# The first 28 slices of a fused attention and gated feed-forward kernel in another hand-given order, with another ring of PSUM banks

## The chip, the cores and the metric

The kernel runs on one core of one Trainium2 chip, as one launch. The metric is the device time of the execution in microseconds (us); lower is better. The core has TensorE (PE, its weight loads shown as PEld), VectorE (DVE), ScalarE (ACT), GpSimd (POOL) and SyncE (SP). Each runs its own instructions in its own order, and they wait for each other by semaphores.

## The reference

```python
# x: [8, 8, 512, 64], state: [8, 8, 32, 64]
scores  = x @ state^T / 8;  a  = softmax(scores);   xread = a @ state     # per batch and head
scores2 = state @ x^T / 8;  a2 = softmax(scores2);  sread = a2 @ x
t = concat([xread, sread], axis=2)        # [8, 8, 544, 64], then heads side by side: [4352, 512]
out = (relu(t @ w_gate) * (t @ w_val)) @ w_out      # 512 -> 1536 -> 512
```

## The kernel before

Matmuls take bf16 and accumulate in the eight PSUM banks (numbers 0 to 7, one tile of 128x512 each). The rows of `xread` are never formed. For each batch the kernel computes U, the product of the state with `w_gate` and `w_val`, and multiplies it by the transposed attention weights (ANS).

The work is cut into **slices**: slice (b, jf) is batch b of 8 and block jf of 12 of the hidden width. A slice is four matmuls of 512 columns into two banks (`gv`, line 290: gate and value), a relu on ACT (line 314), and a multiply on DVE (line 318) that writes `h_sb`. The output projection of a batch is cut into 12 pieces of four matmuls (`out_mms`, line 327); three pieces make one output tile of 128 rows, which ACT copies out of its bank (`fin_x`, line 335) and SP writes to memory (line 339).

**Two ways to set the order.** From slice (2, 4) on, a loop writes the order: a slice, its relu and multiply, one output piece that lags by 18 slices, and then whatever `at` has put behind that slice. For batch 3 that is: the scores of its first heads behind slice (2, 4) and of the others behind (2, 5), U in two blocks behind (2, 7) and (2, 10). The first 28 slices, all that leads up to them and ten output pieces are one long string of words, `program` (line 409). Each word calls one step with its numbers, and each engine meets the instructions in the order of the words. The digits behind `@` are the PSUM banks that the step takes. Steps of the loop take banks from a ring of six (`bank`, line 81), output tiles from banks 6 and 7 in turn.

The words used below (b is a batch):

- `dx.b.part.parts`, `dw`, `ds`, `do`: loads of x, of columns of `w_gate` (dw.0) and `w_val` (dw.1), of the state and of `w_out`, all issued by POOL. The second half of batch 0 is loaded by POOL ahead of the list (line 387), its first half by SP and ACT.
- `xc`, `stc`: casts; `stT`, `sto`: transposed state and its eviction.
- `xT.b.lo.n`, `xo.b.lo.n.engine`: n transposes of blocks of x on PE, and their eviction.
- `sc.b.jp`, `ex`, `nr`, `nx`: scores of half the heads (line 170), exp on ACT (line 177), row sums and reciprocal on DVE (lines 183, 185), scaling on DVE (line 189).
- `aT.b.kc`, `ao`: the attention weights transposed on PE, and evicted to ANS (line 219).
- `c.b.lo.n`, `co.b.lo.n.kc.engine`: U for n columns (tile `upc`) and its evictions (line 285); `u`, `uo`: the same for 512 columns (tile `up`, line 275).
- `gv.b.jf`, `re`, `mu`: the three parts of a slice; `o.0.i`: output piece i of batch 0; `of.0.t`: `fin_x` of its tile t.
- `xd.b` and `ad.b`: the same transposes by DMA, issued by SP: x of batch b into `xT` (line 148), and the attention weights of batch b into ANS (line 197).
- `sr`, `sn`: the matmuls of `sread` (line 233) and their scaling; `xp.b`: POOL's copy of x of batch b into `xa` (line 225), which `sr` reads; `on`: the column of ones there.
- `spin.n.cols`: n matmuls of constants that nobody reads.

Behind the list, the loop's SP steps are transposes of the state (line 122) and of `sn` (line 246); POOL copies the former into `stT` (line 130) ahead of the load of batch 4.

Of the kernel before, what the change touches and what calls it, by code (L numbers as in the profile page):

```python
# [16 lines left out]
def kernel(  # L17
# [51 lines left out]
    stT = const.tile([128, 2, B, H, Ns], BF16, name="stT")  # L69
# [6 lines left out]
    xf, xb, xT, e_sn, a_sn, ANS, U, hsb, sr_sb = {}, {}, {}, {}, {}, {}, {}, {}, {}  # L76
    copy = {"act": nc.scalar.copy, "dve": nc.vector.tensor_copy, "pool": nc.gpsimd.tensor_copy}

    given, turn = [], {"r": 0, "o": 0}

    def bank(name, kind="r"):

        if given:
            n = given.pop(0)
        elif kind == "spare":
            n = 6 + turn["o"] % 2
        else:
            n = (4, 3, 2, 1, 0, 5)[turn["r"] % 6] if kind == "r" else 6 + turn["o"] % 2
            turn[kind] += 1
        return psum.tile([128, 512], FP32, name=name, tag=f"b{n}")  # L90

# [22 lines left out]
    def state_T(g):  # L114
        ps = held["st", g] = bank("stT_ps").bitcast(BF16)[:, 0:512]
        for i in range(4):
            nc.tensor.transpose(ps.rearrange("p (q i m) -> p q i m", i=4, m=8)[:, :, i],
                                st_b[:, g % 3, i].rearrange("p h d -> p (h d)"), id128)
# [31 lines left out]
    def x_T(b, lo, n):  # L150

        if b not in xT:
            xT_alloc(b)
        ps = held["xT", b, lo] = bank("xT_ps").bitcast(BF16)[:, 0:128 * n].rearrange("p (k t) -> p k t", t=128)
        for k in range(n):
            nc.tensor.transpose(ps[:, k], x_blocks(b)[:, lo + k], id128)  # L156
# [5 lines left out]
    def att_sc(b, jp):  # L162
        if b not in e_sn:
            e_sn[b] = att.tile([128, 2, NC, NJ * Ns], BF16, name="e_sn", tag="e_sn", bufs=4)
            a_sn[b] = att.tile([128, 2, NC, NJ * Ns], BF16, name="a_sn", tag="a_sn")
        t = held["sc", b, jp] = bank("sc_ps")
        ps = t.rearrange("p (r c j n) -> p r c j n", r=2, c=NC, j=2)
        for h in range(4 * jp, 4 * jp + 4):
            for k in range(2):
                nc.tensor.matmul(ps[:, h % 2, 2 * k:2 * k + 2, h // 2 % 2], xT[b][:, 2 * h + k], stT[:, :, b, h],  # L170
                                 start=True, stop=True)
# [235 lines left out]
             "c": c_unit, "co": c_out, "u": u_unit, "uo": u_out, "gv": gv, "re": relu, "mu": mult, "o": out_part,  # L407
             "of": fin_x, "xd": x_trans_dma, "ad": att_aT_dma, "xp": x_pad, "sr": sr_mm, "sn": sr_norm}
    program = """
    dx.1.0.2 dx.1.1.2 stc.0.1.dve stc.0.0.dve dw.0.0.128 dw.1.0.128 dw.0.128.128 dw.1.128.128 dw.0.256.256  # L410
    dw.1.256.256 dw.0.512.256 spin.8 stT.0@0 dw.1.512.256 dw.0.768.256 dw.1.768.256 dw.0.1024.256 dw.1.1024.256
    dw.0.1280.256 dw.1.1280.256 dx.2.0.1 ds do.0.6 xc.0.0.act spin.1.256 xT.0.0.4@1 xc.0.1.dve sto.0.0.act
    spin.1.128 xT.0.4.4@2 xo.0.0.4.dve sto.0.1.dve xo.0.4.4.act spin.1 sc.0.0@3 ex.0.0 nr.0.0 spin.1.256 spin.1.128
    xT.0.8.4@4 xT.0.12.4@5 xo.0.8.4.act xo.0.12.4.act spin.1 xT.1.0.8@6 sc.0.1@1 ex.0.1 xo.1.0.8.dve spin.1
    sc.1.0@0 xT.1.8.8@2 stc.1.1.pool stc.1.0.pool do.6.12 spin.1 c.0.0.128@34 nx.0.0 ex.1.0 nr.0.1 xo.1.8.8.act on
    stc.2.0.pool stc.3.1.pool co.0.0.128.0.act co.0.0.128.1.act spin.1 sc.1.1@5 nx.0.1 nr.1.0 aT.0.1@6 aT.0.0@1
    ex.1.1 c.1.128.128@02 ao.0.0.dve ao.0.1.act c.0.128.128@34 c.1.0.128@51 co.0.128.128.0.act gv.0.0@63
    co.1.128.128.1.act co.0.128.128.1.act re.0.0 co.1.128.128.0.act gv.0.1@72 nr.1.1 nx.1.0 co.1.0.128.1.act re.0.1
    nx.1.1 aT.1.0@4 aT.1.1@6 c.0.256.256@01 co.1.0.128.0.dve ao.1.0.dve c.1.256.256@57 co.0.256.256.0.act
    co.1.256.256.0.act co.1.256.256.1.act ao.1.1.dve co.0.256.256.1.dve gv.1.0@46 re.1.0 mu.0.0 mu.0.1 gv.0.2@01  # L420
    gv.1.2@53 mu.1.0 re.0.2 c.0.512.256@72 c.1.512.256@40 re.1.2 mu.1.2 co.0.512.256.1.dve mu.0.2 gv.1.3@65
    gv.1.1@32 co.1.512.256.1.act re.1.3 co.0.512.256.0.act re.1.1 co.1.512.256.0.dve gv.0.3@06 gv.1.5@17 mu.1.1
    mu.1.3 re.0.3 re.1.5 gv.1.4@34 mu.0.3 c.0.768.256@02 re.1.4 mu.1.5 c.0.1024.256@51 c.1.768.256@63
    co.0.768.256.0.act co.0.768.256.1.act mu.1.4 co.1.768.256.1.dve co.1.768.256.0.dve gv.0.4@74 gv.0.6@02 re.0.4
    co.0.1024.256.0.act re.0.6 gv.0.7@37 co.0.1024.256.1.dve mu.0.4 re.0.7 mu.0.6 gv.1.7@65 mu.0.7 re.1.7
    c.0.1280.256@10 c.1.1024.256@43 c.1.1280.256@26 mu.1.7 co.1.1280.256.1.act co.0.1280.256.0.act
    co.0.1280.256.1.dve co.1.1024.256.1.act co.1.1280.256.0.dve gv.0.9@75 co.1.1024.256.0.act gv.0.8@60 gv.0.5@12
    re.0.5 re.0.9 xT.2.0.8@3 re.0.8 mu.0.5 xT.2.8.8@4 xo.2.0.8.dve stT.1@1 sto.1.1.act xo.2.8.8.dve sto.1.0.act
    gv.0.11@72 re.0.11 mu.0.11 mu.0.8 gv.1.9@63 gv.1.11@41 re.1.9 mu.1.9 gv.0.10@76 gv.1.6@20 re.1.11 re.0.10
    sc.2.1@4 gv.1.10@73 re.1.10 ex.2.1 re.1.6 mu.0.10 mu.0.9 o.0.3@6 sc.2.0@5 o.0.4 ex.2.0 o.0.0@7 mu.1.10 mu.1.11  # L430
    u.2.1.1024@43 mu.1.6 nr.2.1 uo.2.1.1024.1.act u.2.1.0@21 u.2.1.512@50 uo.2.1.512.1.act uo.2.1.1024.0.act
    uo.2.1.512.0.act uo.2.1.0.0.act nx.2.1 uo.2.1.0.1.dve o.0.1 o.0.5 stc.2.1.pool dx.3.0.1 xp.1 xp.0 xd.3 sr.1@3
    stc.3.0.pool nr.2.0 sr.0@0 nx.2.0 sn.1 u.2.0.0@14 ad.2 of.0.1.act u.2.0.1024@52 u.2.0.512@63 o.0.2 of.0.0.act
    uo.2.0.0.0.act uo.2.0.512.1.act uo.2.0.512.0.dve o.0.6@6 o.0.7 o.0.9@7 o.0.8 of.0.2.act sn.0 gv.1.8@01
    uo.2.0.0.1.dve uo.2.0.1024.0.dve gv.2.0@45 re.2.0 re.1.8 mu.1.8 gv.2.2@36 xp.3 gv.2.3@40 re.2.2 re.2.3 xp.2
    gv.2.1@31 re.2.1 mu.2.1 mu.2.3 mu.2.0 uo.2.0.1024.1.act mu.2.2
    """
    for word in program.split():
        word, _, banks = word.partition("@")
# [107 lines left out]
```

## Time and profile before

| | |
|---|---|
| three runs | 220.83, 221.51, 221.74 us; median 221.51 |
| profiled execution | 221.39 us, of which the span of the profile is 219.6 us |
| granted TensorE clock, mean | 0.999 |
| PE, DVE, ACT, POOL busy in the span | 97%, 59%, 56%, 19% |
| share of the chain that ended last | PE 92%, DMA 3%, DVE 3% |
| of it, by line | out pieces L327 39%, slices L290 38% |

Times in the profile are microseconds from the start of the span. A PE row such as "x4" merges four matmuls; its length holds the drain of the last, so the time until the next row starts is what the group takes in PE's queue. Four matmuls of a slice or of an output piece take 0.86 us that way. In the chain, each piece is followed back to what released it, and "issue" is time in which an engine waited for nothing that the profile shows. A DMA has two lengths: that of the instruction on the engine that issues it, and the time until its data has landed.

### The profile page before, as it was taken

How to read it: one execution, taken by the hardware profiler on the slowest of the kernel's cores; microseconds unless marked ns; L12 is line 12 of the kernel's file. 1: busy time of each engine (PE TensorE's matmuls, PEld its weight loads, DVE VectorE, ACT ScalarE, POOL GpSimd, SP SyncE). 2: the span in 40 equal slices, each digit the busy share in tenths (PEclk: the TensorE clock that was granted, in tenths of full speed). 3: DMA queues.
4: the chain of work that ended last, by engine and by line, in shares of the span. 5: the costliest groups of instructions: out<-in, count | busy, mean ns of one | idle time of the engine just before them, and what ended most of it. 6: DMA issues, size and time to landing. Idle time of an engine off the chain costs nothing.

```text
span 219.6 us, 4861 instructions
## 1 busy us (share of the span) xinstructions
PE 214.0 (97%) x1957; PEld 105.5 (48%) x1957; DVE 129.4 (59%) x229; ACT 122.8 (56%) x235; POOL 41.7 (19%) x59
## 2 busy tenths in 40 slices
PE   8799999999999999999999999999999999999995
PEld 3454454454444444444444444444444445666544
DVE  5599978862987567665766487648675333222100
ACT  4699887746666565555566555746654544222222
POOL 7874059072143500040003000000000000000000
PEclk9999999999999999999999999999999999999999
DMA  7999999772949883655352105501411122222132
GB/s 164 166 194 198 196 235 174 115 195 81 134 90 145 161 140 96 143 98 102 86 133 79 51 19 142 119 16 48 102 49 54 48 48 49 51 49 74 70 95 99
DMA packets 42215, 23.65 MB, mean 108 GB/s; under 512 B 22640, under 2 KB 37872, under 8 KB 42192
## 3 DMA queue, kind: packets, MB, share of 16 engines
q0 software_dynamic: 16896, 9.05, 30.9%
q1 hardware_dynamic: 24400, 13.54, 23.5%
q10 hardware_dynamic: 896, 0.75, 1.3%
q8 instruction: 15, 0.25, 0.5%
q14 instruction: 8, 0.07, 0.1%
HBM read 18.35 MB, written 8.91 MB: 124 GB/s over the span
## 4 chain that ended last, share of the span: by engine, by line
PE 92%; DMA 3%; DVE 3%; issue 1%; POOL 0%; DVEq 0%; POOLq 0%
PE o_ps L327 39%; PE gv_ps L290 38%; PE gv_ps L307 5%; PE up L263 4%; DMA xb<-in_x_dram 3%; PE upc L263 1%; PE sr_ps L233 1%; PE sc_ps L170 1%; PE o_ps L356 1%; PE xT_ps L156 1%; DVE h_sb L318 1%; DVE a_sn L189 1%; DVE cs L183 1%; DVE xT L159 0%; DVE rc L185 0%
## 5 line engine op out<-in xcount | busy, mean ns | idle before, releaser
L327 PE MATMUL o_ps<-wo_sb,h_sb 128*128 128x512 bf16 x372 | 94.3, 379 | 0.0
L290 PE MATMUL gv_ps<-ans,U 128*128 128x512 bf16 x384 | 93.6, 379 | 0.0
L318 DVE TENSOR_TENSOR h_sb<-gv_ps,g_sb 128x512 bf16<-128x512 f32 x96 | 64.4, 688 | 48.5 <-ACT g_sb L314 47.4
L314 ACT ACTIVATE g_sb<-gv_ps 128x512 bf16<-128x512 f32 (+1 forms) x108 | 62.1, 582 | 44.1 <-PE gv_ps L290 31.5
L290 PEld LDWEIGHTS <-U 128*128 128x128 bf16 x384 | 36.4, 98 | 42.2 <-issue 0.8
L327 PEld LDWEIGHTS <-h_sb 128*128 128x128 bf16 x372 | 35.4, 98 | 40.7 <-issue 2.1
L335 ACT COPY o_sb<-o_ps 128x512 f32<-128x512 f32 x31 | 18.4, 594 | 18.2 <-PE o_ps L327 16.2
L225 POOL COPY xa<-xb 128x1024 bf16<-128x1024 bf16 x16 | 16.1, 1042 | 57.6 <-PE sr_ps L233 52.7
L275 ACT CAST U<-up 128x512 bf16<-128x512 f32 x38 | 19.9, 596 | 12.1 <-PE up L263 12.1
L275 DVE CAST U<-up 128x512 bf16<-128x512 f32 x34 | 21.5, 684 | 3.9 <-PE up L263 3.9
L177 ACT ACTIVATE e_sn<-sc_ps 128x512 bf16<-128x512 f32 x16 | 9.6, 597 | 8.9 <-PE sc_ps L170 8.9
L318 DVE TENSOR_TENSOR hs_sb<-gv_ps,g_sb 128x256 bf16<-128x256 f32 x12 | 5.1, 425 | 15.3 <-PE gv_ps L307 9.2
L183 DVE TENSOR_REDUCE cs<-e_sn 128x16 f32<-128x512 bf16 x16 | 10.9, 679 | 4.4 <-ACT e_sn L177 4.4
L189 DVE TENSOR_TENSOR a_sn<-e_sn,rc 128x512 bf16<-128x512 bf16 x16 | 10.9, 686 | 0.5
L263 PEld LDWEIGHTS <-stT 64*32 64x32 bf16 x560 | 6.5, 90 | 8.7 <-issue 7.5
L285 ACT CAST U<-upc 128x512 bf16<-128x512 f32 (+1 forms) x19 | 8.8, 524 | 1.9 <-PE upc L263 1.9
L170 PEld LDWEIGHTS <-xT 128*128 128x128 bf16 x128 | 5.8, 98 | 4.4 <-DVE xT L159 0.6
L263 PE MATMUL up<-wg_sb,stT 64*32 64x512 bf16 (+1 forms) x168 | 7.3, 349 | 0.2 <-DVE h_sb L318 0.2
L307 PE MATMUL gv_ps<-br,wv_sb 128*128 128x256 bf16 x48 | 7.2, 273 | 0.0
L307 PE MATMUL gv_ps<-br,wg_sb 128*128 128x256 bf16 x48 | 7.2, 273 | 0.0
L263 PE MATMUL up<-wv_sb,stT 64*32 64x512 bf16 (+1 forms) x168 | 7.2, 349 | 0.0
L170 PE MATMUL sc_ps<-stT,xT 128*128 128x64 bf16 x128 | 6.5, 193 | 0.6 <-DVE xT L159 0.3
(53 smaller groups left out, 113.4 us busy)
## 6 DMA issues: line engine op xcount, KB each, us to landing
out_dram<-o_sb SPq DMA_DIRECT2D x26, 256.0 KB, 2.4
xb<-in_x_dram POOLq DMA_DIRECT2D x6, 512.0 KB, 6.5
wo_sb<-in_moe_w_out_dram POOLq DMA_DIRECT2D x2, 768.0 KB, 11.0
out_dram<-o_sb SPq DMA_DIRECT2D x11, 128.0 KB, 2.4
wg_sb<-in_moe_w_gate_dram POOLq DMA_DIRECT2D x5, 256.0 KB, 8.7
wv_sb<-in_moe_w_val_dram POOLq DMA_DIRECT2D x5, 256.0 KB, 9.4
xb<-in_x_dram POOLq DMA_DIRECT2D x3, 256.0 KB, 6.0
st_f<-in_state_dram POOLq DMA_DIRECT2D x1, 384.0 KB, 11.5
```

The source lines that it names most:

```text
L170: nc.tensor.matmul(ps[:, h % 2, 2 * k:2 * k + 2, h // 2 % 2], xT[b][:, 2 * h + k], stT[:, :, b, h], start=True, stop=True)
L183: nc.vector.reduce_sum(out=cs, in_=e_v, axis=AX.X)
L189: {"dve": nc.vector, "pool": nc.gpsimd}[eng].tensor_tensor(out=by_pair(a_sn[b], jp).rearrange("p r (j n) -> p r j n", n=Ns), in0=e_v, in1= ...
L225: nc.gpsimd.tensor_copy(out=v[:, hs], in_=xb[b][:, hs])
L263: nc.tensor.matmul(dst[parity][32 * j:32 * j + 32], stT[r:r + 64, parity, b, 2 * j + parity], wsb[r:r + 64, j, lo:lo + n], start=True, sto ...
L275: copy[eng](out=U[b][:, w, kc, lo:lo + 512], in_=held["u", b, w, lo][kc])
L290: nc.tensor.matmul(ps[w], U[b][:, w, kc, f0:f0 + 128], ANS[b][:, kc].rearrange("p c t -> p (c t)"), start=(kc == 0), stop=(kc == NK - 1))
L307: nc.tensor.matmul(ps[w][:, 0:nt], wsb[:, j, f0:f0 + 128], br[:, j].rearrange("p b n -> p (b n)"), start=(j == 0), stop=(j == NJ - 1))
L314: nc.scalar.activation(out=g_sb[:, 0:n], in_=ps[0][:, 0:n], func=AF.Relu)
L318: nc.vector.tensor_tensor(out=dst, in0=ps[1][:, 0:n], in1=held["g", b, jf][:, 0:n], op=ALU.mult)
L327: nc.tensor.matmul(held["o", b, tsub], src[:, jf, tsub * 128:(tsub + 1) * 128], wo_sb[:, jf], start=(jf == 0), stop=(jf == NF - 1))
L335: copy[eng](out=o_sb, in_=held["o", b, tsub])
```

## The change

The order of the words is another one, the ring of six banks is (2, 3, 5, 1, 0, 4) in place of (4, 3, 2, 1, 0, 5), and the loop's first output tile takes bank 7 in place of 6. The steps are the same but for the spins (16 in place of 17) and the engine of some copies. Among what moves:

- The eviction of batch 0's transposes goes to DVE for three of four pieces, and the scores of its other heads stand ahead of batch 1's transposes.
- POOL issues the same loads in the same sequence up to `do.6.12`; the load of batch 3 follows at once.
- On SP, the transposes by DMA come later. SP's sequence was xd.3, ad.2, and the output DMAs of of.0.1, of.0.0 and of.0.2. It is now the output DMAs of of.0.0 and of.0.1, ad.2, the output DMA of of.0.2, xd.3.

The diff, the removed list cut to its beginning and end:

```diff
-    given, turn = [], {"r": 0, "o": 0}
+    given, turn = [], {"r": 0, "o": 1}
...
-            n = (4, 3, 2, 1, 0, 5)[turn["r"] % 6] if kind == "r" else 6 + turn["o"] % 2
+            n = (2, 3, 5, 1, 0, 4)[turn["r"] % 6] if kind == "r" else 6 + turn["o"] % 2
...
     program = """
-    dx.1.0.2 dx.1.1.2 stc.0.1.dve stc.0.0.dve dw.0.0.128 dw.1.0.128 dw.0.128.128 dw.1.128.128 dw.0.256.256
-    dw.1.256.256 dw.0.512.256 spin.8 stT.0@0 dw.1.512.256 dw.0.768.256 dw.1.768.256 dw.0.1024.256 dw.1.1024.256
-    dw.0.1280.256 dw.1.1280.256 dx.2.0.1 ds do.0.6 xc.0.0.act spin.1.256 xT.0.0.4@1 xc.0.1.dve sto.0.0.act
-    spin.1.128 xT.0.4.4@2 xo.0.0.4.dve sto.0.1.dve xo.0.4.4.act spin.1 sc.0.0@3 ex.0.0 nr.0.0 spin.1.256 spin.1.128
-    xT.0.8.4@4 xT.0.12.4@5 xo.0.8.4.act xo.0.12.4.act spin.1 xT.1.0.8@6 sc.0.1@1 ex.0.1 xo.1.0.8.dve spin.1
-    sc.1.0@0 xT.1.8.8@2 stc.1.1.pool stc.1.0.pool do.6.12 spin.1 c.0.0.128@34 nx.0.0 ex.1.0 nr.0.1 xo.1.8.8.act on
-    stc.2.0.pool stc.3.1.pool co.0.0.128.0.act co.0.0.128.1.act spin.1 sc.1.1@5 nx.0.1 nr.1.0 aT.0.1@6 aT.0.0@1
-    ex.1.1 c.1.128.128@02 ao.0.0.dve ao.0.1.act c.0.128.128@34 c.1.0.128@51 co.0.128.128.0.act gv.0.0@63
-    co.1.128.128.1.act co.0.128.128.1.act re.0.0 co.1.128.128.0.act gv.0.1@72 nr.1.1 nx.1.0 co.1.0.128.1.act re.0.1
-    nx.1.1 aT.1.0@4 aT.1.1@6 c.0.256.256@01 co.1.0.128.0.dve ao.1.0.dve c.1.256.256@57 co.0.256.256.0.act
-    co.1.256.256.0.act co.1.256.256.1.act ao.1.1.dve co.0.256.256.1.dve gv.1.0@46 re.1.0 mu.0.0 mu.0.1 gv.0.2@01
-    gv.1.2@53 mu.1.0 re.0.2 c.0.512.256@72 c.1.512.256@40 re.1.2 mu.1.2 co.0.512.256.1.dve mu.0.2 gv.1.3@65
...
-    re.0.5 re.0.9 xT.2.0.8@3 re.0.8 mu.0.5 xT.2.8.8@4 xo.2.0.8.dve stT.1@1 sto.1.1.act xo.2.8.8.dve sto.1.0.act
-    gv.0.11@72 re.0.11 mu.0.11 mu.0.8 gv.1.9@63 gv.1.11@41 re.1.9 mu.1.9 gv.0.10@76 gv.1.6@20 re.1.11 re.0.10
-    sc.2.1@4 gv.1.10@73 re.1.10 ex.2.1 re.1.6 mu.0.10 mu.0.9 o.0.3@6 sc.2.0@5 o.0.4 ex.2.0 o.0.0@7 mu.1.10 mu.1.11
-    u.2.1.1024@43 mu.1.6 nr.2.1 uo.2.1.1024.1.act u.2.1.0@21 u.2.1.512@50 uo.2.1.512.1.act uo.2.1.1024.0.act
-    uo.2.1.512.0.act uo.2.1.0.0.act nx.2.1 uo.2.1.0.1.dve o.0.1 o.0.5 stc.2.1.pool dx.3.0.1 xp.1 xp.0 xd.3 sr.1@3
-    stc.3.0.pool nr.2.0 sr.0@0 nx.2.0 sn.1 u.2.0.0@14 ad.2 of.0.1.act u.2.0.1024@52 u.2.0.512@63 o.0.2 of.0.0.act
-    uo.2.0.0.0.act uo.2.0.512.1.act uo.2.0.512.0.dve o.0.6@6 o.0.7 o.0.9@7 o.0.8 of.0.2.act sn.0 gv.1.8@01
-    uo.2.0.0.1.dve uo.2.0.1024.0.dve gv.2.0@45 re.2.0 re.1.8 mu.1.8 gv.2.2@36 xp.3 gv.2.3@40 re.2.2 re.2.3 xp.2
-    gv.2.1@31 re.2.1 mu.2.1 mu.2.3 mu.2.0 uo.2.0.1024.1.act mu.2.2
+    xc.0.0.act dx.1.0.2 stc.0.1.dve stc.0.0.dve spin.8 stT.0@0 dx.1.1.2 xc.0.1.dve spin.1.256 xT.0.0.4@1 dw.0.0.128
+    dw.1.0.128 spin.1.128 xT.0.4.4@2 sto.0.1.act dw.0.128.128 xo.0.0.4.dve sto.0.0.act xo.0.4.4.dve dw.1.128.128
+    spin.1.256 sc.0.0@3 dw.0.256.256 dw.1.256.256 dw.0.512.256 dw.1.512.256 ex.0.0 dw.0.768.256 xT.0.8.4@4
+    xo.0.8.4.dve dw.1.768.256 xT.0.12.4@5 xo.0.12.4.act nr.0.0 spin.1 sc.0.1@6 xT.1.0.8@1 spin.2 xT.1.8.8@0 nx.0.0
+    ex.0.1 nr.0.1 nx.0.1 dw.0.1024.256 xo.1.0.8.act sc.1.0@2 xo.1.8.8.dve spin.1 aT.0.0@3 ex.1.0 dw.1.1024.256
+    c.0.0.128@45 c.1.0.128@61 ao.0.0.act co.0.0.128.0.act nr.1.0 sc.1.1@2 aT.0.1@0 ex.1.1 co.0.0.128.1.act spin.1
+    c.0.128.128@34 ao.0.1.dve co.0.128.128.0.act co.1.0.128.0.act co.0.128.128.1.act nx.1.0 nr.1.1 c.1.128.128@02
+    gv.0.0@53 co.1.0.128.1.act re.0.0 gv.0.1@76 re.0.1 nx.1.1 aT.1.0@4 co.1.128.128.1.dve co.1.128.128.0.act
+    aT.1.1@1 ao.1.0.dve c.1.256.256@57 c.0.256.256@20 ao.1.1.dve gv.1.0@41 co.0.256.256.1.act co.0.256.256.0.act
+    re.1.0 co.1.256.256.0.dve co.1.256.256.1.dve mu.0.0 mu.1.0 gv.1.1@50 gv.0.2@27 re.1.1 c.1.512.256@43
+    c.0.512.256@51 re.0.2 mu.1.1 mu.0.2 gv.0.3@20 re.0.3 co.0.512.256.1.act gv.1.2@72 re.1.2 mu.0.1 gv.1.3@61
+    co.1.512.256.1.dve co.1.512.256.0.dve re.1.3 co.0.512.256.0.act gv.1.5@37 re.1.5 mu.1.2 mu.0.3 dw.0.1280.256
+    gv.1.4@46 re.1.4 c.0.768.256@25 mu.1.3 c.1.768.256@03 c.0.1024.256@14 mu.1.5 mu.1.4 co.0.768.256.1.dve
+    dw.1.1280.256 co.0.768.256.0.act co.1.768.256.0.dve co.0.1024.256.0.act gv.0.4@76 co.1.768.256.1.act re.0.4
+    gv.0.6@21 gv.0.7@53 c.0.1280.256@07 re.0.6 co.0.1024.256.1.dve mu.0.4 mu.0.6 c.1.1280.256@42 dx.2.0.1 ds do.0.6
+    re.0.7 co.1.1280.256.0.dve mu.0.7 co.0.1280.256.1.act co.0.1280.256.0.act c.1.1024.256@65 co.1.1280.256.1.act
+    gv.0.9@17 gv.0.10@40 re.0.9 co.1.1024.256.0.dve stc.1.0.pool re.0.10 gv.1.10@32 xT.2.8.8@6 gv.1.7@14 re.1.10
+    re.1.7 mu.0.10 mu.1.10 co.1.1024.256.1.dve mu.1.7 stc.1.1.pool do.6.12 dx.3.0.1 gv.0.11@30 gv.0.8@21 stT.1@5
+    sto.1.0.dve sto.1.1.dve xp.0 stc.2.1.pool re.0.11 xT.2.0.8@4 re.0.8 mu.0.8 mu.0.9 xo.2.0.8.dve mu.0.11
+    xo.2.8.8.act gv.1.9@32 o.0.0@6 gv.0.5@51 re.0.5 re.1.9 o.0.3@7 sc.2.0@4 sc.2.1@5 mu.1.9 mu.0.5 ex.2.0 nr.2.0
+    gv.1.11@03 re.1.11 ex.2.1 gv.1.6@24 o.0.1 re.1.6 u.2.1.512@10 u.2.1.1024@52 mu.1.11 mu.1.6 uo.2.1.512.1.act
+    nx.2.0 uo.2.1.1024.1.dve nr.2.1 u.2.1.0@34 o.0.2 gv.1.8@02 xp.1 stc.3.1.pool on of.0.0.act nx.2.1 o.0.4 re.1.8
+    uo.2.1.0.1.act uo.2.1.512.0.dve uo.2.1.1024.0.act uo.2.1.0.0.act o.0.5 of.0.1.act u.2.0.512@60 u.2.0.1024@41
+    u.2.0.0@53 mu.1.8 uo.2.0.1024.0.dve uo.2.0.512.0.act sr.1@2 sr.0@7 sn.1 o.0.6@6 ad.2 stc.2.0.pool
+    uo.2.0.0.0.act uo.2.0.512.1.act uo.2.0.0.1.act o.0.7 gv.2.2@42 gv.2.1@50 re.2.1 gv.2.0@35 re.2.0 re.2.2 mu.2.2
+    mu.2.0 mu.2.1 o.0.8 of.0.2.act gv.2.3@34 o.0.9@6 stc.3.0.pool re.2.3 xd.3 uo.2.0.1024.1.act sn.0 mu.2.3 xp.3
+    xp.2
```

More of the change, by code (lines that the diff above doesn't have):

```diff
@@ L420 @@
-    co.1.256.256.0.act co.1.256.256.1.act ao.1.1.dve co.0.256.256.1.dve gv.1.0@46 re.1.0 mu.0.0 mu.0.1 gv.0.2@01
-    gv.1.2@53 mu.1.0 re.0.2 c.0.512.256@72 c.1.512.256@40 re.1.2 mu.1.2 co.0.512.256.1.dve mu.0.2 gv.1.3@65
-    gv.1.1@32 co.1.512.256.1.act re.1.3 co.0.512.256.0.act re.1.1 co.1.512.256.0.dve gv.0.3@06 gv.1.5@17 mu.1.1
-    mu.1.3 re.0.3 re.1.5 gv.1.4@34 mu.0.3 c.0.768.256@02 re.1.4 mu.1.5 c.0.1024.256@51 c.1.768.256@63
-    co.0.768.256.0.act co.0.768.256.1.act mu.1.4 co.1.768.256.1.dve co.1.768.256.0.dve gv.0.4@74 gv.0.6@02 re.0.4
@@ L425 @@
-    co.0.1024.256.0.act re.0.6 gv.0.7@37 co.0.1024.256.1.dve mu.0.4 re.0.7 mu.0.6 gv.1.7@65 mu.0.7 re.1.7
-    c.0.1280.256@10 c.1.1024.256@43 c.1.1280.256@26 mu.1.7 co.1.1280.256.1.act co.0.1280.256.0.act
-    co.0.1280.256.1.dve co.1.1024.256.1.act co.1.1280.256.0.dve gv.0.9@75 co.1.1024.256.0.act gv.0.8@60 gv.0.5@12
-    re.0.5 re.0.9 xT.2.0.8@3 re.0.8 mu.0.5 xT.2.8.8@4 xo.2.0.8.dve stT.1@1 sto.1.1.act xo.2.8.8.dve sto.1.0.act
-    gv.0.11@72 re.0.11 mu.0.11 mu.0.8 gv.1.9@63 gv.1.11@41 re.1.9 mu.1.9 gv.0.10@76 gv.1.6@20 re.1.11 re.0.10
```

## The prediction

> **What bounds the kernel now.** I read the page first, for the engine that fills the span:
>
> ```profile
> span 219.6 us, 4861 instructions
> ...
> PE 214.0 (97%) x1957; PEld 105.5 (48%) x1957; DVE 129.4 (59%) x229; ACT 122.8 (56%) x235; POOL 41.7 (19%) x59
> ```
>
> TensorE (PE) has something in flight 97% of the time, DVE and ACT 59% and 56%. So the end moves only by what PE waits, and by spins that stand in its queue ahead of work. Next the chain of waits at the start, to see where PE begins to be full:
>
> ```profile
> 2.66 5.95 DMA xb<-in_x_dram
> ...
> 8.65 0.63 PE xT_ps L156 x8
> ...
> 9.31 0.69 DVE xT L159
> ...
> 11.52 0.69 DVE a_sn L189
> ...
> 13.73 1.83 PE gv_ps L290 x8
> 15.56 0.51 PE aT_ps L205 x8
> 16.07 0.56 PE upc L263 x32
> 16.63 0.54 PE gv_ps L290 x2
> ```
>
> Until 13.4 us the chain runs through the load of batch 1's first half (landed at 8.61) and DVE's softmax steps; from 13.4 us it is PE alone, piece after piece. After that I looked for a piece of the chain that is not PE. There is one, in the first slices after the list:
>
> ```profile
> 59.90 0.88 PE gv_ps L290 x4
> ...
> 61.30 1.29 DVE h_sb L318 x2
> ...
> 62.64 0.41 PE up L263 x7
> 63.05 0.36 PE sr_ps L233 x31
> ```
>
> Three U units (24 matmuls, `up`) start at 61.56 and end at 63.05: 1.49 us. The same three take 0.77 us a batch later (85.94 to 86.72). PE loses 0.72 us there to DVE multiplies that are late, because five of them had piled up behind each other (the timeline has DVE on five multiplies from 54.49 to 57.57). Last I read SyncE's queue (SP), since the change moves two DMA transposes:
>
> ```profile
> 41.49 2.10 SPq L148 DMA_TRANSPOSE xT<-xb  x1
> 44.62 1.24 SPq L197 DMA_TRANSPOSE ans<-a_sn  x1
> ...
> 58.59 0.33 SPq L339 DMA_DIRECT2D out_dram<-o_sb  x1
> 59.01 1.24 SPq L122 DMA_TRANSPOSE hs_sb<-st_b  x1
> ...
> 88.43 0.33 SPq L339 DMA_DIRECT2D out_dram<-o_sb  x1
> 88.86 1.57 SPq L148 DMA_TRANSPOSE xT<-xb  x1
> ```
>
> The columns are start and length of the issue. Their landings come from the answers for the tiles `xT` and then `ans`:
>
> ```profile
> DMA to landing us min/median/max: 4.3/4.4/7.4
> ```
>
> ```profile
> DMA to landing us min/median/max: 3.1/3.1/4.8
> ```
>
> An xT transpose lands 4.3 to 4.4 us after its issue begins in four of five cases, also when an output DMA was issued just before it (the one at 88.86: 4.4). The 7.4 came right behind another transpose. In the kernel before, xT of batch 3 is issued at 41.49 and first read by PE (scores of batch 3) at 55.82: 14 us of cover. ANS of batch 2, issued at 44.62, landed at 47.7 and was needed at about 51.5.
>
> **The head (to gv.1.0).** Same work, one spin fewer (0.22 us, inside PE's waits for landings, so nothing). Batch 0's second half lands at 1.24 + 6.0 = 7.2 in both. Before, ACT evicts both of its quarters (7.72 to 8.79) and the scores sc.0.1 stand behind the transposes of batch 1, which wait for 8.61. After, DVE takes one quarter (7.72 to 8.1), ACT the other (7.94 to 8.52), and sc.0.1 goes first. Exp then starts 0.38 after the eviction, as it did for sc.0.0 (6.23 to 6.61): 8.90, not 9.54. On DVE, by the start-to-start steps of the chain (sum 0.71, reciprocal 0.29, scale 0.61): nr.0.0 from 8.1, nx.0.0 9.1, nr.0.1 9.70, nx.0.1 10.70 to 11.39; before it ended at 12.21. So 0.8 us is won, and then given back. Between it and gv.0.0 ACT now has ao.0.0 (11.89 to 12.47), a first eviction (to 12.75), the exp of sc.1.1 (to 13.30) and then co.0.0.128.1, which frees bank 5 for gv.0.0: 13.56. gv.0.0 starts at 13.60, against 13.66. DVE's second batch (nx.1.1) ends at 15.50 against 15.40, so aT.1.0 waits 0.2 us; gv.1.0 comes at 16.44 against 16.63, with a wait of 0.1 inside. Gain: 0.1 to 0.2.
>
> **The middle (16.6 to about 42).** The same matmuls in another order. With DVE at 0.61 per operation, its queue of 14 operations from 16.63 ends at 25.2, and gv.1.5, gv.0.4 and gv.0.9 wait 0.1 to 0.2 us each for a bank or a copy of U: 0.5 at most, of which the 0.12 us that PE takes at each switch from `upc` to gv (24.24 to 25.09 for 0.66 of work) hides a part. POOL issues the weight loads in the same sequence and with the same waits, so they land as before: the last needed (wv from column 1280) 15.81 + 10.7 = 26.5, used at 27.6; the first half of w_out 19.94 + 14.5 = 34.4, now used at 35.5 instead of 38.5; its second half 38.3, used at 40.3. Margins of 1 to 2 us, so nothing, and 1 us of lateness if the loads share their time otherwise. x of batch 3 is issued one step earlier on POOL, ahead of `on` and the copies into xa. Head and middle together: -0.15, bounds -0.4 and +0.4.
>
> **ad.2 (ANS of batch 2).** On SP it now stands behind the output DMAs of of.0.0 and of.0.1. of.0.1 is ACT's last of six operations after o.0.2 (about 0.52 each). Let F be its end. SP issues its DMA and is free 0.44 later (58.57 to 59.01 in the rows), so ANS lands at F + 0.44 + 3.1 = F + 3.55. PE after F: sr.0 0.3, o.0.6 (its bank is freed by the ACT copy after of.0.1), o.0.7 at 0.86 each; gv.2.2 is reached at F + 2.3. It waits 1.25 us. Bounds: 1.0 (ACT not late at of.0.1) and 2.95 (landing 4.8). I take 1.25: five of six landed in 3.1 to 3.2, none behind another transpose here.
>
> **xd.3 (xT of batch 3).** It now stands on SP behind the output DMA of of.0.2, which needs o.0.8. Let T be the end of o.0.8. ACT's copy runs T + 0.2 to T + 0.79 (0.59, as at 57.98), SP gives the output DMA and is at xd.3 at T + 1.23, the data lands at T + 5.6. PE after T: gv.2.3, o.0.9, then from the steady loop gv of (2,4) and an out piece, 4 x 0.864 = 3.46, then the scores of batch 3. They wait 5.6 - 3.46 = 2.15, with the wake-up 2.2 us. The pair "output DMA, then xT" is just the row at 88.43 and 88.86, so I take its 4.4; with 7.4 it is 5.2. Behind the scores PE holds gv of (2,5) and all that follows, so ACT and DVE run dry too. Behind xd.3 SP holds the state transposes, whose POOL copies hold back the load of batch 4: to 54.5 + 2.1 + 2.9 + 1.3 = 60.8 from 54.73. With 8.5 to land that is 69.3, and its transpose is issued at 67.01 + 2.6 = 69.6: covered.
>
> The Trainium skill, "DMA: Bandwidth & Descriptors", "Latency and other measured facts", gives a DMA transpose an effective 261 GB/s; 512 KB would move in an estimated 2.0 us and ANS in 1.0, and if that were all, neither wait would exist and the sum would be 220.5. The rows disagree: 4.4 and 3.1 from issue to landing.
>
> **Ring and hand-over.** The list ends with the banks that the new ring wants next: gv of (2,4) takes 2 and 3, last read by mu.2.2 and re.2.3, done 1 us earlier. After that a ring in another order is the same ring. What changes is the backlog: the list now leaves one multiply (mu.2.3) open where it left four, and the wait at the scores gives DVE 2 us more. The 0.72 us at the U units goes: -0.7 (bounds 0 and -0.72).
>
> **Sum.** Against the profiled execution's own 221.4 (span 219.6 plus 1.8 around it; the median of the runs is 0.1 above): -0.15 + 1.25 + 2.2 - 0.7 = +2.6, so 224.0.
>
> **Rivals.**
> - Faster: the transposes are ready in time. It needs xT within 2.2 us of issue, ANS within 1.85. For it: their issues last 1.6 to 2.1 and 1.24 us, and if the data were there when the issue ends, both waits vanish. Against: no landing under 4.3 or 3.1. Then 221.4 - 0.15 - 0.7 = 220.5, at best 220.3. Chance 0.13.
> - Only one of the waits is seen, since other lateness ahead of it on PE (a late bank at o.0.6, a late gv.2.3) uses the same time: 222.7 with xT's alone, 221.8 with ANS's alone. Chance 0.12.
> - The clock drops in the gap. The first eight spins are 0.43 us apart, 0.22 later: 3.4 us at half speed after idleness, or 1.7 us lost: 225.7. Against: nothing after 4 us runs at half speed, but no gap in this trace is over 0.54 us. Chance 0.05. The Trainium skill, "TensorE: Matmul & The Clock Gate", "Part 1: The HAM clock gate", wants an idle window of about 3.4 us for it; by that rule 2.2 us is too short and the time stays 224.0; no row here has such a gap.
> - A transpose lands slowly, as two did: 225.7 (ANS 4.8) or 227.0 (xT 7.4). Chance 0.06.
> - The order does not do what it says, for batch 0 lands elsewhere than computed: both kernels wait for it and shift alike; the bounds of the head hold it.
>
> **Numbers.** The forecast keeps 0.64, with its own range 223.0 to 225.4. From 221.8 to 226.2 are the forecast, the one-wait cases, the clock and the slow ANS; left out are the faster rival and xT at 7.4. A difference under 0.5% (1.1 us) can't be told from none here. Faster by more: part of the first rival, 0.07. Within: the rest of it and ANS's wait alone, 0.13. Slower: 0.80.
>
> **What would show it.** PE's scores of batch 3 waiting about 2 us for the DMA into xT, with SP's xT issue right behind the third output DMA; gv on batch 2 waiting about 1.2 us for the DMA into ans; gv.1.0 near 16.4; `up` after the list in 0.8 us. I am wrong if xT or ANS is there when PE comes, or if PE reaches that place some microseconds later than the walk has it.

## The result, and the profile after

The changed kernel takes 225.26 us (median of six runs, 223.83 to 225.96) against 221.46 (six runs): 1.0169 times, 95% interval 1.0149 to 1.0189. It is slower by 3.8 us; 224.0 was forecast, with 221.8 to 226.2 around it. The profiled execution took 225.69, its span 223.9, which is 4.3 more than before.

From the page, the totals and the granted clock in 40 slices of 5.6 us:

```profile
span 223.9 us, 4835 instructions
...
PE 213.4 (95%) x1927; PEld 106.4 (48%) x1956; DVE 131.3 (59%) x232; ACT 121.9 (54%) x232; POOL 41.8 (19%) x59
...
PEclk9999999999889999999999999999999999999999
```

PE's share fell to 95%, and two slices have a clock under nine tenths, which no slice had before. The chain of waits through the hand-over from the list to the loop shows where PE stood still:

```profile
46.62 3.15 DMA ans<-a_sn
...
49.90 2.75 PE gv_ps L290 x12
52.65 0.86 PE o_ps L327 x4
53.51 0.86 PE gv_ps L290 x4
...
54.62 4.40 DMA xT<-xb
59.02 0.05 issue
59.07 0.41 PE sc_ps L170 x8
...
60.18 1.73 PE o_ps L327 x4
```

Both DMA transposes are now on the chain, from their issue to their landing: 3.15 us for ANS, 4.40 us for xT. PE had ended o.0.7 at 48.7 and waited to 49.90, 1.2 us; it had ended the out piece behind slice (2,4) at 56.8 and waited to 59.07, 2.27 us. SP's queue shows why they were issued there (start and length of the issue):

```profile
43.65 2.92 SPq L339 DMA_DIRECT2D out_dram<-o_sb  x2
46.62 1.39 SPq L197 DMA_TRANSPOSE ans<-a_sn  x1
54.16 0.34 SPq L339 DMA_DIRECT2D out_dram<-o_sb  x1
54.62 1.98 SPq L148 DMA_TRANSPOSE xT<-xb  x1
```

Each follows an output DMA by the 0.4 to 0.5 us that the issue of that DMA takes; x of batch 3 had landed at 41.9 and the attention weights for ANS were ready two microseconds before that issue. The last row of the chain above has a second loss: an out piece of 1.73 us in place of 0.86. The stages behind the gap show it (length, then busy time of PE, PEld, DVE, ACT and POOL, granted clock, DMA share, GB/s):

```profile
60.00:61.00 1.00, 0.95 (x4) 0.45 (x4) 0.82 (x2) 0.60 (x2) 0.94 (x3) 0.68 0.01 0
61.00:62.00 1.00, 1.00 (x9) 0.44 (x8) 0.96 (x3) 0.05 (x1) 0.79 (x1) 0.50 0.00 0
62.00:63.00 1.00, 1.00 (x10) 0.44 (x8) 0.45 (x1) 1.00 (x2) 0.00 (x0) 0.50 0.71 31
63.00:64.00 1.00, 1.00 (x4) 0.38 (x3) 0.90 (x2) 0.63 (x2) 0.00 (x0) 0.62 0.73 51
```

The missing clock adds up to 0.32 + 0.50 + 0.50 + 0.38 = 1.7 us of PE's time: 3.4 us at half clock. Five of the six runs have a mean clock of 0.991 or 0.992 and take 225.2 to 226.0; the sixth has 0.999 and takes 223.83.

The gains are there too. The three U units, in PE's timeline of the kernel before and then of this one (`sr_ps` starts where they end):

```profile
61.56 0.41 PE L263 MATMUL up<-wg_sb,stT 64*32 64x512 bf16 x8
...
62.64 0.41 PE L263 MATMUL up<-wg_sb,stT 64*32 64x512 bf16 x7 [0.19 <-DVE h_sb L318]
62.98 0.43 PE L233 MATMUL sr_ps<-xa,e_sn 128*32 128x65 bf16 x32
```

```profile
66.49 0.41 PE L263 MATMUL up<-wg_sb,stT 64*32 64x512 bf16 x8
66.72 0.40 PE L263 MATMUL up<-wv_sb,stT 64*32 64x512 bf16 x8
66.93 0.40 PE L263 MATMUL up<-wg_sb,stT 64*32 64x512 bf16 x8
67.26 0.43 PE L233 MATMUL sr_ps<-xa,e_sn 128*32 128x65 bf16 x32
```

They took 1.42 us and take 0.77. Without its two waits PE would have reached the scores of batch 3 at 59.07 - 2.27 - 1.2 = 55.6, against 55.82 before. So: 1.2 + 2.27 + 1.7 - 0.65 - 0.2 = 4.3 us, the whole of it.

### The profile page after: what moved, and what is told of

Same layout as the page of the kernel before. It is cut to its first block, busy times and chain, and to the rows that moved or that the text cites. A ratio compares the mean times of both kernels' runs of the same rounds, so it can differ in the third digit from the quotient of the medians.

```text
span 223.9 us, 4835 instructions
## 1 busy us (share of the span) xinstructions
PE 213.4 (95%) x1927; PEld 106.4 (48%) x1956; DVE 131.3 (59%) x232; ACT 121.9 (54%) x232; POOL 41.8 (19%) x59
## 4 chain that ended last, share of the span: by engine, by line
PE 88%; DMA 6%; issue 2%; POOL 2%; DVE 0%; POOLq 0%
PE o_ps L327 37%; PE gv_ps L290 37%; PE gv_ps L307 5%; PE up L263 4%; DMA wv_sb<-in_moe_w_val_dram 3%; DMA xT<-xb 2%; PE sc_ps L170 1%; DMA ans<-a_sn 1%; PE upc L263 1%; PE o_ps L356 1%; PE sr_ps L233 1%; POOL xb L394 1%; POOL wg_sb L103 1%; PE xT_ps L156 0%; POOL wv_sb L103 0%
## 5 line engine op out<-in xcount | busy, mean ns | idle before, releaser
L327 PE MATMUL o_ps<-wo_sb,h_sb 128*128 128x512 bf16 x356 | 92.4, 381 | 2.2 <-issue 1.7
L275 ACT CAST U<-up 128x512 bf16<-128x512 f32 x39 | 20.4, 597 | 11.6 <-PE up L263 11.6
L275 DVE CAST U<-up 128x512 bf16<-128x512 f32 x33 | 20.9, 684 | 4.5 <-PE up L263 4.5
L285 ACT CAST U<-upc 128x512 bf16<-128x512 f32 (+1 forms) x17 | 7.7, 507 | 1.3 <-PE upc L263 1.3
L285 DVE CAST U<-upc 128x512 bf16<-128x512 f32 (+1 forms) x11 | 6.9, 657 | 0.2 <-PE upc L263 0.2
L394 POOL DMA_DIRECT2D xb<-in_x_dram x8 | 6.8, 850 | 1.2 <-DMA wg_sb<-in_moe_w_gate_dram 1.2
```

The costliest lines, as they stand in the source:

```text
L275: copy[eng](out=U[b][:, w, kc, lo:lo + 512], in_=held["u", b, w, lo][kc])
L285: copy[eng](out=U[b][:, :, kc, lo:lo + n], in_=held["c", b, lo][kc])
L327: nc.tensor.matmul(held["o", b, tsub], src[:, jf, tsub * 128:(tsub + 1) * 128], wo_sb[:, jf], start=(jf == 0), stop=(jf == NF - 1))
```

## The experiments

Theory A: the loss is the two late transposes and the clock behind the longer gap, and the new order without them gains. Theory B: the new order or ring loses by itself, and the two waits are only where PE's lateness shows. On the clock: one gap does it, or it takes both, or something else.

Experiments 1 to 4 ran on one chip and 5 to 8 on another, each set beside 23 runs of the kernel before. So kernels of different sets are compared by their ratios to it, and only one run of each kernel is profiled. The chip may matter for the clock: on the first, none of the 55 runs had a mean clock under 0.999; on the second, one of the 23 runs of the kernel before had 0.991 (222.96 us).

**1. Both transposes early** (`e1_both_early`). Words moved in the list; PE, DVE, ACT and POOL keep their order.

```diff
-... gv.1.6@24 o.0.1 ...            of.0.0.act nx.2.1 o.0.4 ...
+... gv.1.6@24 xd.3 o.0.1 ...       of.0.0.act nx.2.1 ad.2 o.0.4 ...
-... o.0.6@6 ad.2 stc.2.0.pool ...  re.2.3 xd.3 uo.2.0.1024.1.act ...
+... o.0.6@6 stc.2.0.pool ...       re.2.3 uo.2.0.1024.1.act ...
```

> The changed kernel with two words moved: xd.3 ahead of o.0.1 and ad.2 right behind nx.2.1. Only SP's sequence differs (xT, output DMA, ANS, two output DMAs); PE, ACT, DVE and POOL have the same instructions in the same order. Theory A (the whole loss is the two late transposes and the clock that drops behind the longer gap; the new order alone gains): both waits gone, no second at half clock, U units in 0.77 us: 221.46 - 0.72 - 0.3 for the head = 220.4. Theory B (the new order or ring loses by itself and the two waits are only where its lateness shows): 222 to 224, with waits of PE for ACT or DVE in the place of the DMA waits.

Measured: 220.67 us (220.05 to 222.08) against 221.07, ratio 0.9982 (0.9963 to 1.0001). The 4 us of loss are gone with SP's order alone, which excludes B. But in the profiled run only one wait went. SP's queue and PE's timeline of that profile:

```profile
43.34 2.09 SPq L148 DMA_TRANSPOSE xT<-xb  x1
45.48 0.94 SPq L339 DMA_DIRECT2D out_dram<-o_sb  x1
46.47 1.31 SPq L197 DMA_TRANSPOSE ans<-a_sn  x1
```

```profile
49.97 2.75 PE L290 MATMUL gv_ps<-ans,U 128*128 128x512 bf16 x12 [1.07 <-DMA ans<-a_sn]
```

x of batch 3 took 11.3 us to land here, 9.4 in the changed kernel's profile. SP stood at xT until 43.34, and what stood behind it, ANS too, was late once more. The miss is mine: I moved a transpose ahead of a load that had not landed and forgot what queues behind it. The profiled run (221.86 us) is one of the two longest of the twelve; the other ten took 220.05 to 220.96. How often the wait for ANS comes is not shown; the median leaves little room for it.

**2. Only xT early** (`e2_xd_early`): of these edits, those with `xd.3`.

> The changed kernel with only xd.3 moved ahead of o.0.1; ad.2 stays behind the output DMA of of.0.1. Theory A: the wait for ANS alone is left, 1.1 to 1.2 us, and a gap of that length does not drop the clock (mean 0.999): 220.4 + 1.2 = 221.6. Theory B: within 0.5 of e1_both_early, since the lateness shows elsewhere. If the gap of 1.2 us is enough for the clock: 223.3.

Measured: 221.68 us, ratio 1.0025 (1.0006 to 1.0043), mean clock 0.999 or 1.000 in all ten runs. Against experiment 5, which has neither wait, the one for ANS is worth 1.0025 - 0.9966 = 0.6%, 1.3 us (by the two intervals, 0.7 to 1.9). In the profiled run, 222.34 us, PE was idle for 1.59 us there; the clock did not drop.

**3. Only ANS early** (`e3_ad_early`): those with `ad.2`.

> The changed kernel with only ad.2 moved behind nx.2.1; xd.3 stays behind the output DMA of of.0.2. Theory A: the wait for xT alone is left, 2.2 us: 222.6 where the clock holds, 224.2 where it drops. If the gap at xT alone makes the clock drop, most runs show a mean clock near 0.992 and 224.2; if it takes both gaps, all show 0.999 and 222.6.

Measured: 222.85 us, ratio 1.0075 (1.0060 to 1.0089), clock 1.000 in all five runs. The wait and its size, from PE's timeline, and the stage behind it:

```profile
57.84 0.41 PE L170 MATMUL sc_ps<-stT,xT 128*128 128x64 bf16 x8 [2.11 <-DMA xT<-xb]
```

```profile
60.00:64.00 4.00, 4.00 (x40) 1.75 (x38) 3.93 (x7) 2.17 (x4) 0.55 (x1) 1.00 0.66 73
```

The same gap as in the changed kernel, 1.2 us earlier in the run, at full clock afterwards. Against experiment 5 it is worth 1.0075 - 0.9966 = 1.1%, 2.4 us (1.8 to 3.0). So both waits have the size that was forecast, and something more than the gap's length decides about the clock: its place in the run, the other gap, or the chip.

**4. The gap at the scores filled with spins** (`e4_fill8`). A function `fill(n)` issues n matmuls of constants into a tile of bank 7:

```diff
     first, lag = 2 * NF + 4, 18
+    at(2, 4, fill, 8)
```

> The changed kernel with 8 spins of 512 columns (1.73 us of PE time) between the out piece behind slice (2,4) and the scores of batch 3, into bank 7, read by nobody. PE would wait there for xT anyway (2.2 us), so the spins cost nothing by themselves; the gap shrinks to about 0.5 us. If the gap drops the clock: mean clock 0.999 in every run and 223.7, 1.6 below the changed kernel. If the drop has another cause: 225.3 and 0.992 as before.

Measured: 224.01 us (223.62 to 225.06), ratio 1.0136, clock 0.999 or 1.000 in all five runs.

```profile
56.46 1.91 PE L477 MATMUL fill_ps<-const-bfloat16-1.0 128*128 128x512 bf16 x8
58.78 0.41 PE L170 MATMUL sc_ps<-stT,xT 128*128 128x64 bf16 x8 [0.41 <-DMA xT<-xb]
```

By the ratios this is 0.7 us faster than the changed kernel (1.0136 against 1.0169), although xT is as late as it was and PE does more. It agrees with idle time as the cause of the drop but does not show it: experiment 3, on the same chip, left the gap open and lost no clock either.

**5. ANS early, then xT** (`e5_ad_then_xd`). As in 1, but both words stand behind `nx.2.1`:

```diff
-... of.0.0.act nx.2.1 o.0.4 ...
+... of.0.0.act nx.2.1 ad.2 xd.3 o.0.4 ...
```

> The changed kernel with ad.2 and then xd.3 right behind nx.2.1, so SP has: output DMA, ANS, xT, two output DMAs. In e1_both_early x of batch 3 landed at about 43.3 us, SP waited for it with xT, and ANS behind it was late again by 1.1 us. Theory A (nothing but the two transposes and the clock costs time): no wait over 0.3 us at gv.2.2 or at the scores of batch 3, and e3_ad_early less its gap: 222.85 - 2.25 = 220.6, at least 0.1% under the kernel before. Theory B (the new order costs by itself): 221.1 or more.

Measured: 220.77 us (219.96 to 221.39) against 221.42, ratio 0.9966 (0.9945 to 0.9987). It beats both kernels. PE's timeline has no wait at either place, and the U units take 0.82 us (62.13 to 62.95) with no gap ahead of them:

```profile
49.48 2.75 PE L290 MATMUL gv_ps<-ans,U 128*128 128x512 bf16 x12
...
56.39 0.40 PE L170 MATMUL sc_ps<-stT,xT 128*128 128x64 bf16 x8
...
62.13 0.41 PE L263 MATMUL up<-wg_sb,stT 64*32 64x512 bf16 x8
...
62.95 0.43 PE L233 MATMUL sr_ps<-xa,e_sn 128*32 128x65 bf16 x32
```

By the medians 0.65 us is won against the kernel before, and 1.42 - 0.82 = 0.60 would be the U units alone. The profiled run does not show the sum: it is the longest of the twelve (221.39), and its span is that of the profile before, 219.6. PE reaches the scores of batch 3 at 56.39, 0.57 later than before, and that is lost in the head. From the chain of waits:

```profile
1.24 6.57 DMA xb<-in_x_dram
...
16.02 0.62 PE aT_ps L205 x8
```

Batch 0's second half landed at 7.81 here, and at 6.75 in the changed kernel's profile. So what the new head is worth on the whole stays open. Why the U units are short is plainer. DVE's row sums follow the start of the first scores of batch 3 by 1.06 us here (56.39 to 57.45) and by 1.67 before (55.82 to 57.49), when DVE came to them straight from its five multiplies. Here, and then before:

```profile
57.45 0.69 DVE L183 TENSOR_REDUCE cs<-e_sn 128x16 f32<-128x512 bf16 x1 [0.83 <-ACT e_sn L177]
```

```profile
54.49 3.08 DVE L318 TENSOR_TENSOR h_sb<-gv_ps,g_sb 128x512 bf16<-128x512 f32 x5 [1.41 <-ACT g_sb L314]
57.49 0.68 DVE L183 TENSOR_REDUCE cs<-e_sn 128x16 f32<-128x512 bf16 x1
```

**6. The same with the old ring** (`e6_old_ring`).

```diff
-            n = (2, 3, 5, 1, 0, 4)[turn["r"] % 6] if kind == "r" else 6 + turn["o"] % 2
+            n = (4, 3, 2, 1, 0, 5)[turn["r"] % 6] if kind == "r" else 6 + turn["o"] % 2
```

> e5_ad_then_xd with the loop's ring put back to (4, 3, 2, 1, 0, 5); the list and its banks stay, and so does the first output bank 7. Theory A (a ring in another order is the same ring but for the hand-over): slice (2,4) then takes bank 4 (freed by mu.2.3) and 3: it waits 0.2 to 0.5 us once, the U units still take under 0.9 us, and the time is 220.6 to 221.1. Theory C (the new ring itself takes the 0.72 us at the U units away): the U units take 1.3 us or more and the time is 221.3.

Measured: 222.1 us (221.39 to 223.07), ratio 1.0034: 1.3 us more than with the new ring, and outside what I expected. The U units keep 0.82 us, so C is out. (PE's stop at the hand-over also gave DVE time; but in experiment 5 there is no such stop, and DVE waits for ACT at those row sums all the same.) The hand-over is what I undersized. PE and DVE in the timeline:

```profile
52.55 1.89 DVE L318 TENSOR_TENSOR h_sb<-gv_ps,g_sb 128x512 bf16<-128x512 f32 x3 [4.86 <-ACT g_sb L314]
...
54.36 0.16 DVE L240 RECIPROCAL rr<-sr_ps 128x2 f32<-128x2 f32 x1
54.55 0.29 DVE L242 TENSOR_TENSOR sn<-sr_ps,rr 128x128 bf16<-128x128 f32 x1
54.76 0.68 DVE L318 TENSOR_TENSOR h_sb<-gv_ps,g_sb 128x512 bf16<-128x512 f32 x1
...
55.49 1.02 PE L290 MATMUL gv_ps<-ans,U 128*128 128x512 bf16 x4 [1.07 <-DVE h_sb L318]
```

Slice (2,4) then takes bank 4, which mu.2.3 reads, and on DVE that multiply stands behind three others and sn.0. The new ring hands over two banks that are free.

**7. The changed kernel with ANS's gap filled** (`e7_fill_ans`), so that xT's gap stays at its place in time:

```diff
-... o.0.7 gv.2.2@42 ...
+... o.0.7 fl.5@4 gv.2.2@42 ...     (five spins into bank 4)
```

> The changed kernel with 5 spins of 512 columns (1.08 us) ahead of gv.2.2, into bank 4, read by nobody, so that PE has nearly no gap while ANS lands; the gap of 2.2 us at the scores of batch 3 stays at the same place in time. If that gap does it alone, and only its place in time kept e3_ad_early from the drop: mean clock 0.992 and 225.2 in most runs. If it takes both gaps: clock 0.999 and 223.7 in all runs.

Measured: 225.2 us, ratio 1.0170 (1.0141 to 1.0199). Four of six runs have a clock of 0.991 or 0.992 and 225.2 to 226.4, two have 0.999 and take 224.4 and 224.7. In the profile the gap is again 2.3 us, and half clock follows:

```profile
59.79 0.41 PE L170 MATMUL sc_ps<-stT,xT 128*128 128x64 bf16 x8 [2.13 <-DMA xT<-xb]
```

```profile
61.00:62.00 1.00, 1.00 (x4) 0.42 (x3) 0.93 (x3) 0.32 (x1) 0.96 (x2) 0.50 0.01 0
```

It does not take both gaps. One of 2.3 us is enough, though not in every run. In experiment 3, where it comes 2 us earlier in the profile and on the other chip, it did it in none of five; these runs do not separate place from chip.

**8. xT later still** (`e8_xd_later`): experiment 3 with xd.3 out of the list and behind the loop's first state transpose.

```diff
+    at(2, 4, x_trans_dma, 3)       # and "xd.3" out of the list
```

> e3_ad_early with xd.3 moved from the list behind the loop's first state transpose on SP, so that xT of batch 3 is issued some 1.7 us later and lands at least that much later; the gap on PE becomes 4 us or more, the only one. If a single gap drops the clock once it is long enough (2.2 us was not): a stretch of about 3.4 us at half clock behind it, and 222.85 + 1.8 + 1.7 = 226.3, more if the transposes collide. If a single gap never does it: clock 0.999 and 224.6.

Measured: 225.69 us (224.73 to 227.24), ratio 1.0203 (1.0167 to 1.0239). In this profile PE was ready at 56.07 (the out piece starts at 55.21 and takes 0.86), so the gap is 3.4 us; it is 1.15 longer than in the changed kernel, not 1.8, for the state transpose took SP 1.24 us to issue here (1.71 in the changed kernel, where it stands behind xT):

```profile
59.49 0.41 PE L170 MATMUL sc_ps<-stT,xT 128*128 128x64 bf16 x8 [3.26 <-DMA xT<-xb]
```

Five of six runs lost clock, two of them twice as much (0.985); one kept it (1.000). Against experiment 3 the ratios differ by 1.0203 - 1.0075 = 1.3%, 2.8 us, which is 1.15 for the gap and 1.7 for the clock.

On this one chip the clock can now be set against the gap: with the gap at the scores open (experiments 7 and 8) nine of twelve runs lost clock, without it (5, 6 and the kernel before) four of 47. So the gap brings the drop, though not in every run, and now and then one comes without it.

## Why the prediction was right, and where it was short

- **The place, the two waits and their sizes: right.** ANS 1.25 us forecast, 1.2 measured; xT 2.2 forecast, 2.27 measured. The landings were those of the rows of before, 3.15 and 4.40, and SP's delay behind an output DMA 0.46. Experiments 2, 3 and 5 show each alone and none. By the figure of the Trainium skill ("DMA: Bandwidth & Descriptors", "Latency and other measured facts") xT would take an estimated 2.0 us; 4.40 was measured from issue to landing.
- **The U units: right.** -0.7 forecast, -0.65 measured, and -0.60 in experiment 5, where PE had not stood still before them. It is the shorter backlog on DVE, as said, not the ring (experiments 5 and 6). The 1.49 us of the prediction takes its start from PE's timeline and its end from the chain; the timeline alone has 1.42, so the most that could be won was 0.65 and not 0.72.
- **The ring: right in sign, no term of its own.** I wrote that the banks are free at the hand-over and put nothing down for it. The old ring with the new list costs 1.3 us by the medians (experiment 6), and its profile has 1.07 us of idle time there.
- **The head and the middle: -0.15 forecast, -0.2 in this profile, in part by luck.** gv.1.0 came at 16.36, 16.44 forecast. But the walk had landings of one profile: batch 0's second half lands here at 6.8, not 7.2, and the chain runs through another load. The chain of waits, start:

```profile
6.37 6.59 DMA wv_sb<-in_moe_w_val_dram
12.96 0.04 issue
13.00 0.36 PE upc L263 x24
13.36 1.83 PE gv_ps L290 x8
```

  A load of weights sets the time, where the walk had ACT's queue. In experiment 5's profile the same order ran 0.57 us later than the kernel before, outside the bound of +0.4.
- **The clock: the step that failed.** I gave this rival 5 in 100, and it came in five of six runs. Without it the forecast of 224.0 would have been close: the one run without it took 223.83. The median lies just inside the forecast's own range (223.0 to 225.4) by a loss that the forecast left out, and that is luck. Its price was right, 1.7 us. Its chance came from a trace that has no gap of that length, which is no evidence, and from the rule in the Trainium skill ("TensorE: Matmul & The Clock Gate", "Part 1: The HAM clock gate") that an idle window of about 3.4 us is needed. The runs here differ: nine of twelve runs of the two kernels whose profiles show a gap of 2.3 us (this one and experiment 7) lost the clock. What the Trainium skill says there of the length of the slow stretch agrees: 3.4 us. It calls the window free-running; a drop that comes in some runs and not in others fits that, but no run here shows where a window begins, so what decides in a given run stays open. So does why one of the twelve runs of experiment 5, two of the twelve of experiment 6 and one of the 23 of the kernel before beside them lost as much clock; those runs were not profiled.
- **Two readings that are off, without weight in the sum.** ANS of batch 2 was needed before at 50.6, not 51.5: slice (1, 8) starts at 49.77 and slice (2, 0) 0.86 later. And the 0.12 us at a switch to gv is that of the timeline (24.24 to 25.02); the 25.09 beside it is the chain's.

## What to carry to other kernels

Cost a DMA transpose from issue to landing, and put it on its queue: its start is the time at which everything ahead of it on SP has been issued, output DMAs that wait for late copies included. Before moving one earlier, ask whether its source has landed, for a transpose that waits holds up all behind it (experiment 1). And price a PE gap of 2 us or more with the clock that may follow: here 2.27 us of waiting cost up to 4, with the 1.7 of the clock.

## What the runs showed of the hardware that was not expected

- A gap of 2.3 us on PE, in a kernel that otherwise keeps it full, was followed by 3.4 us at a granted clock of 0.50 in the two profiles that have it at that place, and nine of the twelve runs of these two kernels had the mean clock that goes with it. No safe length is shown: gaps of 0.4 to 1.6 us (experiments 2 and 4) did it in none of fifteen runs on one chip, but experiment 6, with 1.07 us in its profile, lost clock in two of twelve on the other.
- The clock does not drop in the gap. It is granted in full there and falls after PE has work again: 1.3 us after in the changed kernel (0.68 for the stretch from 60 to 61 us is half clock from 60.36 on, and the scores start at 59.07), 1.0 after, by the same working, in the profiles of experiments 7 and 8.
- The load of batch 3 took 8.5 to 11.3 us in profiles of kernels that issue it at nearly the same time. An order computed for one landing has to stand the others.
